# Attention sums with queries in the rows for the first two groups, dummy matmuls at the start, and a bank rule in the planner

## The chip, the cores and the metric

The kernel runs on one core of a Trainium2 chip. The time is that of the device, in microseconds, for one execution; the median of three runs before the change is 550.58 us (549.27 to 551.24). The engines are TensorE (PE, matmuls; its weight loads are shown as PEld), VectorE (DVE), ScalarE (ACT), GpSimd (POOL), and SyncE (SP), which only issues DMAs. PE writes to PSUM, eight banks that DVE and ACT can read and POOL cannot.

## The reference

Three parts follow one another. Window attention: 2 batches x 8 heads, 768 positions, 64 dimensions; a query sees the first 4 keys (sinks) and the 128 keys up to its own. Then a dense feed-forward layer over 1536 rows. Then a routed layer: eight experts, each row to its best one.

```python
scores = scale * np.matmul(q, k.transpose(0, 1, 3, 2))
keep = is_sink | in_window                       # pos < n_sink; 0 <= rel < window
scores = np.where(keep, scores, -1e9)
a = np.exp(scores - np.max(scores, axis=-1, keepdims=True))
a = a / (np.sum(a, axis=-1, keepdims=True) + 1e-09)
x = np.matmul(a, v)                              # then to rows of 512
h = x @ w_in; x = np.maximum(0.01 * h, h) @ w_out
# routed: softmax gate over 8 experts, argmax, x + gate * (relu(x @ w1[e]) @ w2[e])
```

## The kernel before

The 1536 rows are six groups of 256 (g = 0 to 5; 0 to 2 are the first batch). The attention of a group has eight items: four head pairs p times two query tiles qt of 128. The dense layer of a group is 16 chunks f: twelve matmuls of 256 columns (line 845), a leaky ReLU that goes ACT, DVE, ACT, DVE (lines 856 to 859), and six matmuls of 512 columns (line 866). The weights of the dense layer are read as raw words, decoded by DVE and split in two parts (lines 737 to 741, 701, 708) once, during group 0. While the chunks of a group run, the attention of the next one is worked in between. The routed part begins some 430 us into the run.

All work is written as operations with an engine, a cost, a priority `pr`, what they read and write, and the buffers that they hold. `Plan.run` goes through planned time with these costs and starts on each engine the ready operation of the best priority whose buffers fit; the resulting order is the program's order on each engine. Buffers have tags with a number of slots: for PSUM `acc` 2, `h` 2, `S` 1, `T` 2, `PV` 1. `T` takes whatever PE turns (keys `pk`, queries `pq`, probabilities `tt`). Plan.gap gives the time from one operation to one that depends on it.

Groups 0 and 1 (`self.whole`) work in full fp32; group 2 does so for the scores; the others split numbers in two parts. An item of group 0 or 1 runs like this, in `item`: the score matmul of each head (line 578) with queries `qz` that `prep` copied from the turned bank with the factor -0.125 (lines 465 on DVE, 468 on ACT; 454 and 456 are the keys and the sink keys); mask and minimum on DVE (line 585); exponential with its sum on ACT (line 588); the sum's reciprocal `sm` on DVE (592, 593); the probabilities are scaled by it, on ACT (line 597) in group 1 and for the second head in group 0, on POOL (line 600) for the first head in group 0; PE turns them (line 616, and 638 for the sink columns from the third query block on); ACT copies them to `AT` (line 620); and PE sums the values (line 655). There the weights are the values of a head, 64 columns beside 64 cleared ones (POOL clears them, line 365), the moving operand is the 128 turned probabilities, and the sum comes out with dimensions in the rows, as the dense layer wants it. ACT copies it (line 661), and DVE makes the second part (line 662). Where sinks count, each head has one matmul more, against `vs` (cleared on POOL, line 405).

The values are loaded by two DMAs a block, one for each head of the pairs (line 349), the keys and queries by one a block (line 343). In groups 3 to 5 the turned keys are copied by ACT and subtracted by DVE (lines 501 and 503), both for two heads.

Of the kernel before, what the change touches and what calls it, by code (L numbers as in the profile page):

```python
# [47 lines left out]
C_TR = 114.0  # L48
# [3 lines left out]
class Buf:  # L52
    __slots__ = ("tag", "shape", "dtype", "tile", "left", "state", "first", "loose")

    def __init__(self, tag, shape, dtype):
        self.tag, self.shape, self.dtype = tag, shape, dtype
        self.tile = None
        self.left, self.first = 0, 1 << 60
        self.state = {}


class Op:
    __slots__ = ("i", "eng", "cost", "fn", "pr", "after", "wait", "ready", "bufs", "lat", "start")


class Plan:
# [12 lines left out]
    def __init__(self, slots, any_order=()):  # L79
        self.any_order = any_order  # L80
# [16 lines left out]
    def op(self, eng, cost, fn, r=(), w=(), pr=0.0, lat=0.0, hold=(), after=()):  # L97
# [28 lines left out]
        for d in deps:  # L126
            d.after.append(o)
        bufs.update(dict.fromkeys(hold))
# [7 lines left out]
    def run(self, emit_alloc):  # L136
# [12 lines left out]
        def fits(o):  # L149
            need = {}  # L150
# [13 lines left out]
        while future:  # L164
# [18 lines left out]
            for eng in sorted(ready):  # L183
# [42 lines left out]
class Arm:  # L226
# [4 lines left out]
    def __init__(self, tc, io, cst, scr, xg, window_attention):  # L231
# [19 lines left out]
        self.p = Plan({**base, **attn, **late}, ("T", "acc"))  # L251
# [78 lines left out]
    def blocks(self, g, b, qp):  # L330
# [5 lines left out]
        def ld(t, a, p0, p1):  # L336
# [3 lines left out]
            if t != "v":  # L340
                eng, dma = ("ACT", nc.scalar) if g == 0 and t == "k" and p0 == 0 else ("SP", nc.sync)
                x = self.raws[t, a // 2]
                P.op(eng, C_DMA, lambda: dma.dma_start(
                    out=x.tile[:, a % 2, 128 * p0:128 * p1].rearrange("p (h d) -> p h d", d=64), in_=src.rearrange("h p d -> p h d")),
                    w=[(x, (a % 2, p)) for p in range(p0, p1)], pr=pr, lat=64 * n * 1024 / 200.0)
                return
            x = self.raws[t, a]
            for h in range(2):
                P.op("SP", C_DMA, lambda h=h: nc.sync.dma_start(
                    out=x.tile[:, p0:p1, h, 64 * h:64 * h + 64], in_=io["v"][b, 2 * p0 + h:2 * p1:2, 128 * a:128 * a + 128, :].rearrange("h p d -> p h d")),  # L350
                    w=[(x, (h, 0))], pr=pr, lat=32 * n * 1024 / 200.0)

        new = range(2 * qp, 2 * qp + 2)
        for t in "qk":
            self.raws[t, qp] = P.buf("w", [128, 2, 512])
        for p0, p1 in ((0, 1), (1, self.KD)) if g == 0 else ((0, self.KD),):
# [3 lines left out]
            if p0 == 0:  # L360
                for a in new:

                    x = self.raws["v", a] = P.buf("w", [128, self.KD, 2, 128])
                    for h in range(2):
                        P.op("POOL", 100 + 0.9 * 256, lambda x=x, h=h: nc.gpsimd.memset(x.tile[:, :, h, 64 - 64 * h:128 - 64 * h], 0.0), w=[(x, (h, 1))], pr=pr)
                    if g:
                        ld("v", a, 0, self.KD)
        if g == 0:
            for a in new:
                ld("v", a, 0, self.KD)  # L370
# [21 lines left out]
    def sinks_v(self, g, b, whole):  # L392
# [3 lines left out]
        vs = self.vs = P.buf("vs", [128, self.KD, 2, 128], F32 if whole else F32R)  # L396
        if whole:
            def ld():
                for h in range(2):
                    nc.sync.dma_start(out=vs.tile[h:32:2, :, h, 64 * h:64 * h + 64], in_=src(h))  # L400
# [4 lines left out]
            P.op("POOL", 1000, lambda: nc.gpsimd.memset(vs.tile, 0.0), w=[vs], pr=pr - 7)  # L405
# [27 lines left out]
    def prep(self, g, qp, p, whole):  # L433
# [21 lines left out]
        if qp == 0:  # L455
# [4 lines left out]
        P.op("PE", 2 * C_TR, lambda: [nc.tensor.transpose(pq.tile[:, j, :], flat("q", 2 * qp + j), idt) for j in range(2)],  # L460
             r=[part("q", 2 * qp + j) for j in range(2)], w=[pq], pr=pr, hold=[kT])
# [91 lines left out]
    def item(self, g, qp, p, qt, whole):  # L553
# [40 lines left out]
        for h in range(2):  # L594
            if g == 1 or g == 0 and h:

                P.op("ACT", c_act(ncol, False), lambda h=h: nc.scalar.activation(out=A.tile[:, 0:ncol, h], in_=A.tile[:, 0:ncol, h], func=AF.Copy, scale=sm.tile[:, h:h + 1]),
                     r=[sm], w=[(A, h)], pr=pr)
                continue
# [26 lines left out]
        if whole:  # L626
            vb = [self.raws["v", 2 * qp - 1 + j] for j in js]
            rd = [*AT, *vb]
            vblk = lambda i, h: vb[i].tile[:, p, h, :]
# [17 lines left out]

        def pvmm():
            for h in range(2):
# [3 lines left out]
                for n, (l, r) in enumerate(mm):  # L653
                    to = pv.tile[:, 0, 0:128] if whole else pv.tile[:, h, :]
                    nc.tensor.matmul(out=to, lhsT=l, rhs=r, start=n == 0 and not (whole and h), stop=n == len(mm) - 1 and (h == 1 or not whole))  # L655

        P.op("PE", (nj + 2 * sink) * (213 if whole else c_mm(256)), pvmm, r=rd, w=[pv], pr=pr)
        if whole:
            xT = self.xt[g]
            x = lambda i: xT.tile[:, i, p, 128 * qt:128 * qt + 128]  # L660
            P.op("ACT", c_act(128, True), lambda: nc.scalar.activation(out=x(0), in_=pv.tile[:, 0, 0:128], func=AF.Copy), r=[pv], w=[(xT, (p, 0, qt))], pr=pr)
            P.op("DVE", c_dve(128), lambda: nc.vector.tensor_tensor(out=x(1), in0=pv.tile[:, 0, 0:128], in1=x(0).bitcast(F32), op=ALU.subtract),
# [781 lines left out]
```

## Time and profile before

| | |
|---|---|
| median of three runs | 550.58 us |
| the profiled execution | 549.7 us |
| its span, first to last instruction | 548.0 us |
| PE busy | 517.1 us (94%) |
| DVE busy | 411.6 us (75%) |
| ACT busy | 344.3 us (63%) |
| POOL busy | 164.5 us (30%) |

The span is what the trace covers; the execution's own time is 1.7 us longer. Shares of busy time are averages over a start, a stretch with the weights' decoding, the other groups, and the routed part, and each has other limits. A matmul's end is modelled, so where PE reads full one looks at the distance from one start to the next. An fp32 matmul of groups 0 and 1 leaves two records.

### The profile page before, as it was taken

The page shows a single profiled execution, that of the slowest core. Times are in us where ns is not written, and L with a number is a line of the kernel's source. Part 1 is how long each engine was busy: PE and PEld are TensorE (multiplying, and loading weights), DVE is VectorE, ACT ScalarE, POOL GpSimd, SP SyncE. Part 2 cuts the span into 40 slices and gives each one's busy share as a digit, 9 for nine tenths or more (in the row PEclk, how much of TensorE's full clock was granted, in tenths as well). Part 3 has the DMA queues.
Part 4 walks back from the last instruction along what each step waited for, and adds up shares of the span by engine and source line. Part 5 has one row for each costly group of instructions (what it writes and reads, how often), then busy time and mean ns, then how long its engine had stood idle before and what let it go on. Part 6 is the DMA issues. An engine that isn't in the chain of part 4 may idle for free.

```text
span 548.0 us, 10288 instructions
## 1 busy us (share of the span) xinstructions
PE 517.1 (94%) x3341; PEld 452.8 (83%) x3341; DVE 411.6 (75%) x1168; ACT 344.3 (63%) x899; POOL 164.5 (30%) x288
## 2 busy tenths in 40 slices
PE   3889999999998999989999999999999999999994
PEld 2779899888887999878988889999998778888883
DVE  4889999998667677687777776675765587788781
ACT  3998865655576556676566676465656377765760
POOL 4332012230155134332433333211131033455331
PEclk9999999999999999999999999999999999999998
DMA  8998443630110211131112230104565359988750
GB/s 158 298 333 279 156 144 97 198 105 25 64 42 22 69 27 42 41 93 35 45 46 50 49 85 18 26 1 178 169 185 191 116 179 372 315 280 300 245 193 19
DMA packets 83806, 72.44 MB, mean 132 GB/s; under 512 B 56563, under 2 KB 64755, under 8 KB 83744
## 3 DMA queue, kind: packets, MB, share of 16 engines
q1 hardware_dynamic: 81456, 70.54, 42.3%
q0 software_dynamic: 1600, 1.04, 0.6%
q8 instruction: 28, 0.46, 0.3%
q14 instruction: 34, 0.28, 0.2%
q10 hardware_dynamic: 688, 0.13, 0.1%
HBM read 65.40 MB, written 10.51 MB: 139 GB/s over the span
## 4 chain that ended last, share of the span: by engine, by line
PE 74%; DVE 11%; ACT 7%; issue 3%; POOL 2%; DMA 2%; POOLq 0%; SPq 0%; ACTq 0%; DVEq 0%
PE h L845 19%; PE acc L866 15%; PE acc L1103 8%; PE h L1086 4%; PE PV L655 4%; PE T L616 3%; PE S L1086 2%; PE PV L1086 2%; PE S L582 2%; DVE C L671 2%; ACT P L588 2%; PE S L866 2%; PE PV L866 2%; DVE kT L503 1%; PE T L1096 1%
## 5 line engine op out<-in xcount | busy, mean ns | idle before, releaser
L845 PE MATMUL h<-x,w 128*128 128x256 f32 x1128 | 154.7, 286 | 0.3 <-DVE x L708 0.2
L845 PEld LDWEIGHTS h<-x,w 128*128 128x128 f32 x1128 | 144.1, 190 | 4.9 <-DVE w L708 0.6
L866 PE MATMUL acc<-w,gh 128*128 128x512 f32 x308 | 100.2, 406 | 0.0
L588 ACT ACTIVATE P<-P,s 128x272 f32<-128x272 f32 (+1 forms) x96 | 50.1, 523 | 27.6 <-DVE s L585 26.2
L600 POOL TENSOR_SCALAR P<-P,s 128x272 f32<-128x272 f32 (+1 forms) x72 | 36.6, 520 | 90.1 <-DVE s L593 77.4
L866 PE MATMUL acc<-w,gl 128*128 128x512 f32 x156 | 61.3, 393 | 0.0
L856 ACT ACTIVATE t<-h 128x256 f32<-128x256 f32 x94 | 35.6, 379 | 38.2 <-PE h L845 37.8
L866 PEld LDWEIGHTS acc<-w,gh 128*128 128x128 f32 x308 | 53.2, 189 | 7.6
L857 DVE TENSOR_TENSOR h<-h,t 128x256 f32<-128x256 f32 x94 | 40.2, 428 | 21.8 <-ACT t L856 21.2
L708 DVE TENSOR_TENSOR w<-wm,w 128x1024 fp32r<-128x1024 f32 x36 | 49.3, 1376 | 3.8 <-ACT w L701 3.2
L701 ACT ACTIVATE w<-wm 128x1024 fp32r<-128x1024 f32 x44 | 45.1, 1057 | 5.1 <-PE h L845 2.9
L859 DVE TENSOR_TENSOR gl<-h,gh 128x256 fp32r<-128x256 f32 x92 | 38.6, 419 | 10.2 <-ACT gh L858 8.9
L858 ACT ACTIVATE gh<-h 128x256 fp32r<-128x256 f32 x92 | 34.9, 379 | 17.4 <-DVE h L857 16.6
L585 DVE CUSTOM_DVE_ANT_0 P<-S,mk 128x272 f32<-128x272 f32 (+1 forms) x70 | 28.9, 413 | 14.7 <-PE S L582 10.2
L701 ACT ACTIVATE w<-wf 128x512 fp32r<-128x512 f32 x52 | 32.0, 626 | 11.1 <-DVE wf L741 8.8
L866 PEld LDWEIGHTS acc<-w,gl 128*128 128x128 f32 x156 | 29.3, 188 | 6.8 <-DVE gl L859 0.2
L708 POOL TENSOR_TENSOR w<-wm,w 128x1024 fp32r<-128x1024 f32 x8 | 19.7, 2461 | 41.8 <-ACT w L701 21.1
L616 PE MATMUL T<-idt,P 128*128 128x128 f32 x152 | 26.9, 293 | 3.8 <-DVE kT L503 2.9
L672 POOL TENSOR_TENSOR xr<-C 128x128 f32<-128x128 f32 x32 | 15.6, 488 | 47.2 <-DVE C L671 46.8
L708 DVE TENSOR_TENSOR w<-wf,w 128x512 fp32r<-128x512 f32 x42 | 28.8, 693 | 0.7 <-ACT w L701 0.7
L616 PEld LDWEIGHTS T<-idt,P 128*128 128x128 f32 x152 | 22.3, 205 | 8.5 <-issue 4.2
L622 ACT ACTIVATE AT<-T 128x256 fp32r<-128x256 f32 x60 | 20.1, 382 | 12.1 <-PE T L616 11.3
(274 smaller groups left out, 1105.9 us busy)
## 6 DMA issues: line engine op xcount, KB each, us to landing
wm<-in_moe_w_dram SPq DMA_DIRECT2D x44, 512.0 KB, 3.8
w<-in_moe_w_in_dram SPq DMA_DIRECT2D x14, 512.0 KB, 7.4
w<-in_moe_w_out_dram SPq DMA_DIRECT2D x14, 512.0 KB, 6.5
wf<-in_moe_w_dram SPq DMA_DIRECT2D x20, 256.0 KB, 4.4
vs<-in_moe_w_dram SPq DMA_DIRECT2D x10, 512.0 KB, 5.7
rq<-in_q_dram SPq DMA_DIRECT2D x56, 64.0 KB, 5.8
out_dram<-x SPq DMA_DIRECT2D x12, 256.0 KB, 2.5
rk<-in_k_dram SPq DMA_DIRECT2D x24, 96.0 KB, 2.2
```

What stands on the lines that cost most here:

```text
L588: P.op("ACT", 280 + 0.83 * ncol, lambda h=h: nc.scalar.activation(out=A.tile[:, 0:ncol, h], in_=A.tile[:, 0:ncol, h], func=AF.Exp, scale=- ...
L600: P.op("POOL", 245 + 0.83 * ncol, lambda h=h: nc.gpsimd.tensor_scalar(out=A.tile[:, 0:ncol, h], in0=A.tile[:, 0:ncol, h], scalar1=sm.tile[ ...
L616: nc.tensor.transpose(tt.tile[:, 2 * j + h, :], A.tile[:, o:o + 128, h], c["idt"])
L701: nc.scalar.activation(out=at(0), in_=view(src.tile), func=AF.Copy)
L708: P.op(lo, {"DVE": c_dve(n), "POOL": c_pool2(n)}[lo], lambda: eng[lo].tensor_tensor(out=at(1), in0=view(src.tile), in1=at(0).bitcast(F32), ...
L845: nc.tensor.matmul(out=h.tile, lhsT=wi.tile[:, a, 128 * k:128 * k + 128], rhs=xT.tile[:, b, k, :], start=k == 0 and n == 0, stop=k == self ...
L856: P.op("ACT", c_act(256, True), lambda: nc.scalar.activation(out=t.tile, in_=h.tile, func=AF.Copy, scale=0.01), r=[h], w=[t], pr=fast)
L857: P.op("DVE", c_dve(256), lambda: nc.vector.tensor_tensor(out=h.tile, in0=h.tile, in1=t.tile, op=ALU.max), r=[t], w=[h], pr=fast)
L859: P.op("DVE", c_dve(256), lambda: nc.vector.tensor_tensor(out=gl.tile, in0=h.tile, in1=gh.tile.bitcast(F32), op=ALU.subtract), r=[h, gh], ...
L866: nc.tensor.matmul(out=acc[i].tile, lhsT=a.tile[:, q], rhs=wo.tile[:, b, :], start=first and n == 0, stop=last and n == 2)
L1086: nc.tensor.matmul(out=hp[a].tile, lhsT=xt.tile[:, i, k, :], rhs=w1[k][j].tile[:, 512 * a:512 * a + 512], start=k == 0 and n == 0, stop=k ...
L1103: nc.tensor.matmul(out=yp.tile, lhsT=gt.tile[:, a, 2 * n + j, :], rhs=w2[n][b].tile[:, 512 * j:512 * j + 512], start=n == 0 and j == 0 and ...
```

## The change

In groups 0 and 1 the sums are made the other way round: the turned probabilities are the weights, the 64 value columns of a head are the moving operand, and the sum comes out with queries in the rows. One matmul of 128 columns adds the sinks of both heads. Since the queries are now in the rows, the reciprocal scales the sum (ACT, 64 columns a head) in place of the probabilities; PE turns the scaled sum, and copy and second part are made from there. Values need no cleared halves, so they are loaded by one DMA a block. In group 0's first pair ACT makes both query copies. PE gets seven dummy matmuls at the start and five behind the first turned queries. The planner holds back an operation from a PSUM buffer while another engine is planned at it, and a little beyond.

```diff
+        def fits(o):
+            if any(b.tag in self.banks and b.by != o.eng and b.until > now and b not in o.held for b in o.bufs):
+                return False
...
+                for b in got.bufs:
+                    if b.tag in self.banks and b not in got.held:
+                        b.by, b.until = eng, end + (195.0 if eng == "PE" else 150.0)
+                        later(b.until, "idle", None)
...
-        self.p = Plan({**base, **attn, **late}, ("T", "acc"))
+        self.p = Plan({**base, **attn, **late}, ("T", "acc"), self.psum_tags)
...
-        for t in "qk":
+        for t in "qkv":
             self.raws[t, qp] = P.buf("w", [128, 2, 512])
...
+        if g == 0 and p == 0:
+            self.warm(5, pr, [turned])
         for h in range(2):
-            if g == 0 and h:
+            if g == 0 and p and h:
                 P.op("DVE", c_dve(256), ...
...
-        for h in range(2):
-            if g == 1 or g == 0 and h:
-                P.op("ACT", c_act(ncol, False), ... scale=sm.tile[:, h:h + 1]
-                continue
+        for h in [] if whole else range(2):
             P.op("POOL", 245 + 0.83 * ncol, ...
...
+        def rows():
+            mm = [(pv.tile[:, 0, 0:128], wz.tile, vs.tile[:, p, :])] if sink else []
+            mm += [(pv.tile[:, 0, 64 * h:64 * h + 64], at(i, h), vblk(i, h)) for h in range(2) for i in range(len(js))]
+            for n, (to, l, r) in enumerate(mm):
+                nc.tensor.matmul(out=to, lhsT=l, rhs=r, start=n == 0, stop=n == len(mm) - 1)
...
-        P.op("PE", (nj + 2 * sink) * (213 if whole else c_mm(256)), pvmm, r=rd, w=[pv], pr=pr)
+        P.op("PE", (nj + sink) * 222 if whole else (nj + 2 * sink) * c_mm(256), rows if whole else pvmm, r=rd, w=[pv], pr=pr)
         if whole:
+            y = P.buf("qT", [128, 128])
+            def scale():
+                for h in range(2):
+                    nc.scalar.activation(out=y.tile[:, 64 * h:64 * h + 64], in_=pv.tile[:, 0, 64 * h:64 * h + 64], func=AF.Copy, scale=sm.tile[:, h:h + 1])
+            P.op("ACT", 2 * c_act(64, True), scale, r=[pv, sm], w=[y], pr=pr)
+            tx = P.buf("T", [128, 128])
+            P.op("PE", C_TR, lambda: nc.tensor.transpose(tx.tile, y.tile, c["idt"]), r=[y], w=[tx], pr=pr)
...
+        if self.fast:
+            self.spare = self.p.buf("acc", [128, 512])
+            self.warm(7, -100)
...
+    def warm(self, n, pr, after=()):
+        nc, ones, x = self.nc, self.c["ones"], self.spare
+        many = ones.rearrange("p (o n) -> p o n", o=1).to_broadcast([128, 4, 128])
+        self.p.op("PE", 10 * n, lambda: [nc.tensor.matmul(out=x.tile.rearrange("p (o n) -> p o n", o=4), lhsT=ones, rhs=many, start=True, stop=True) for _ in range(n)],
+                  w=[x], pr=pr, after=after)
```

The rule changes the planned times and with them the order on all engines, up to the routed part; behind it the order is the same. Three places follow, each before and after. In the rows a tile's number stands behind its name.

PE, from the start to the first turned probabilities, before (keys and queries `w` are turned into `T`; `S` and `h` take scores; `acc` takes turned probabilities):

```order
L450 MATMUL T_151<-idt,w_127 128x128 x2
L460 MATMUL T_155<-idt,w_131 128x128 x2
L578 MATMUL S_171<-kT_152,w_141 128x128
L578 MATMUL h_176<-kT_152,w_141 128x128
L578 MATMUL h_181<-kT_152,w_141 128x272
L578 MATMUL S_188<-kT_152,w_141 128x272
```

The same after; `acc_129` takes the dummies:

```order
L814 MATMUL acc_129<-ones 128x512
L442 MATMUL T_154<-idt,w_127 128x128 x2
L452 MATMUL T_158<-idt,w_139 128x128 x2
L814 LDWEIGHTS ones
L814 MATMUL acc_129<-ones 128x512
...
L572 MATMUL S_175<-kT_155,w_152 128x128
L572 MATMUL h_180<-kT_155,w_152 128x128
L572 MATMUL h_183<-kT_155,w_152 128x272
L572 MATMUL S_192<-kT_155,w_152 128x272
```

Seven dummies stand ahead of the first turning and five between the queries' turning and the first score.

PE in group 1 before, one item's sum and the work behind it (`PV` is the sum, `AT` the turned probabilities, `w_242` and `w_261` the values, `C` and `vs` the sinks, `h` a chunk of the dense layer):

```order
L655 MATMUL PV_1017<-AT_987,w_242 128x128
L655 MATMUL PV_1017<-AT_987,w_261 128x128
L655 MATMUL PV_1017<-C_129,vs_148 128x128
L655 MATMUL PV_1017<-AT_987,w_242 128x128
L655 MATMUL PV_1017<-AT_987,w_261 128x128
L655 MATMUL PV_1017<-C_129,vs_148 128x128
L578 MATMUL S_1033<-kT_760,w_141 128x272
L845 MATMUL h_1042<-x_251,w_984 128x256 x12
L616 MATMUL T_1060<-idt,P_956 128x128 x4
L638 MATMUL T_1067<-idt,P_956 32x128
```

After (`qT_986` is the scaled sum):

```order
L642 MATMUL PV_967<-vs_141,C_137 128x128
L642 MATMUL PV_967<-w_150,AT_901 128x64
L642 MATMUL PV_967<-w_252,AT_901 128x64
L642 MATMUL PV_967<-w_150,AT_901 128x64
L642 MATMUL PV_967<-w_252,AT_901 128x64
L605 MATMUL T_977<-idt,P_909 128x128 x4
L627 MATMUL T_990<-idt,P_909 32x128
L572 MATMUL S_992<-kT_813,w_152 128x272
L859 MATMUL h_998<-x_281,w_934 128x256 x12
L664 MATMUL T_1020<-idt,qT_986 128x128
```

Five matmuls take the place of six, and the scaled sum is turned behind the next probabilities, a score and a chunk.

PE in a later group before, from a turning of keys to the third turning, which takes the keys' bank again (`rk` keys, `rq` queries, `P` probabilities; `T` has two slots):

```order
L494 MATMUL T_3428<-idt,rk_3224 128x128 x3
L681 MATMUL T_3436<-idt,rq_3363 128x128 x2
L866 MATMUL acc_2582<-w_1820,gh_3391 128x512 x2
L866 MATMUL acc_2582<-w_1820,gl_3394 128x512
L866 MATMUL acc_2583<-w_1820,gh_3391 128x512 x2
L866 MATMUL acc_2583<-w_1820,gl_3394 128x512
L845 MATMUL h_3462<-x_3432,w_367 128x256 x3
L616 MATMUL T_3470<-idt,P_3375 128x128 x4
```

After:

```order
L488 MATMUL T_3441<-idt,rk_3229 128x128 x3
L685 MATMUL T_3449<-idt,rq_3347 128x128 x2
L880 MATMUL acc_2724<-w_1741,gh_3411 128x512 x2
L880 MATMUL acc_2724<-w_1741,gl_3415 128x512
L880 MATMUL acc_2725<-w_1741,gh_3411 128x512 x2
L880 MATMUL acc_2725<-w_1741,gl_3415 128x512
L859 MATMUL h_3473<-x_1962,w_1899 128x256 x12
L605 MATMUL T_3488<-idt,P_3393 128x128 x4
```

Here twelve matmuls of a chunk stand ahead of the third turning in place of three.

## Rows read from the trace of the kernel before

**Rows 1.** The page: busy time by engine, and tenths in 40 slices
```profile
PE 517.1 (94%) x3341; PEld 452.8 (83%) x3341; DVE 411.6 (75%) x1168; ACT 344.3 (63%) x899; POOL 164.5 (30%) x288
...
PE   3889999999998999989999999999999999999994
```

**Rows 2.** Stretches: length, busy us (instructions) by engine, clock, DMA share, GB/s
```profile
0.00:10.00 10.00, 2.02 (x7) 1.38 (x8) 3.59 (x15) 2.32 (x5) 6.16 (x26) 1.00 0.80 140
...
20.00:30.00 10.00, 8.48 (x59) 7.09 (x59) 9.46 (x37) 8.91 (x31) 3.49 (x7) 1.00 1.21 295
...
60.00:70.00 10.00, 10.00 (x71) 9.20 (x70) 9.70 (x29) 8.12 (x24) 0.22 (x1) 1.00 0.09 36
```

**Rows 3.** Timeline of PE at the start: start, us, instruction [idle before, its end]
```profile
9.33 0.77 PE L578 MATMUL S<-kT,w 128*128 128x128 f32 x2 [2.19 <-ACT w L468]
...
11.23 1.11 PE L578 MATMUL S<-kT,w 128*128 128x272 f32 x2
...
13.71 0.52 PE L616 MATMUL acc<-idt,P 128*128 128x128 f32 x2 [0.89 <-POOL P L600]
...
16.19 0.62 PE L578 MATMUL S<-kT,w 128*128 128x272 f32 x2
```

**Rows 4.** Timeline of the other engines at the start
```profile
2.24 0.19 POOL L1368 MEMSET ones<- 128x128 bf16 x1
...
7.03 0.18 ACT L456 ACTIVATE ks<-T 128x16 f32<-128x16 f32 x1
...
8.35 0.43 DVE L465 TENSOR_SCALAR w<-T 64x256 f32<-64x256 f32 x1
8.81 0.38 ACT L468 ACTIVATE w<-T 64x256 f32<-64x256 f32 x1 [1.60 <-DVE w L465]
...
10.47 0.41 ACT L588 ACTIVATE P<-P,s 128x128 f32<-128x128 f32 x1 [1.28 <-DVE s L585]
...
11.95 0.55 ACT L588 ACTIVATE P<-P,s 128x272 f32<-128x272 f32 x1 [0.55 <-DVE s L585]
...
17.89 0.41 DVE L737 TENSOR_SCALAR wf<-w 128x512 int32<-128x512 int32 x1
```

**Rows 5.** The chain that ended last: start, us, what
```profile
56.49 1.39 PE acc L866 x6
57.88 1.34 PE PV L655 x12
...
140.92 0.87 PE T L929 x8
```

**Rows 6.** Timeline of PE: fp32 records with 128 and with nine columns
```profile
57.72 0.61 PE L655 MATMUL PV<-AT,w 128*128 128x128 f32 x4
...
146.65 0.61 PE L951 MATMUL T<-fold,wl 18*128 18x9 f32 x4
```

**Rows 7.** ACT's groups to 95 us: count, busy us, mean ns, idle before
```profile
L597 ACT ACTIVATE P<-P,s 128x272 f32<-128x272 f32 x20 | 10.1, 544 | 1.2 <-DVE s L593 1.1
...
L661 ACT ACTIVATE x<-PV 128x128 fp32r<-128x128 f32 x16 | 4.2, 265 | 3.9 <-PE PV L655 3.9
...
L597 ACT ACTIVATE P<-P,s 128x128 f32<-128x128 f32 x4 | 1.6, 400 | 0.0
...
L456 ACT ACTIVATE ks<-T 128x16 f32<-128x16 f32 x4 | 0.7, 170 | 0.0
```

**Rows 8.** PE's waits at 120 to 440 us: total, times, longest
```profile
PE T L616 <- DVE kT L503: 2.9, 7, 0.6
...
PE T L638 <- DVE qT L684: 1.3, 4, 0.6
```

**Rows 9.** Timeline around two turnings of keys, at 239 and 302 us
```profile
239.60 0.71 PE L616 MATMUL T<-idt,P 128*128 128x128 f32 x4 [0.61 <-DVE kT L503]
...
301.85 0.98 ACT L501 ACTIVATE kT<-T 64x384 fp32r<-64x384 f32 x2
...
302.87 1.12 DVE L503 TENSOR_TENSOR kT<-T,kT 64x384 fp32r<-64x384 f32 x2
```

More of the change, by code (lines that the diff above doesn't have):

```diff
@@ L52 @@
 class Buf:
-    __slots__ = ("tag", "shape", "dtype", "tile", "left", "state", "first", "loose")
+    __slots__ = ("tag", "shape", "dtype", "tile", "left", "state", "first", "loose", "by", "until")
     def __init__(self, tag, shape, dtype):
@@ L58, in __init__ @@
         self.left, self.first = 0, 1 << 60
+        self.by, self.until = None, 0.0
         self.state = {}
 class Op:
-    __slots__ = ("i", "eng", "cost", "fn", "pr", "after", "wait", "ready", "bufs", "lat", "start")
+    __slots__ = ("i", "eng", "cost", "fn", "pr", "after", "wait", "ready", "bufs", "lat", "start", "held")
 class Plan:
@@ L339, in ld @@
             src = io[t][b, heads, 128 * a:128 * a + 128, :]
[L340 to L347, printed above, removed]
-            for h in range(2):
-                P.op("SP", C_DMA, lambda h=h: nc.sync.dma_start(
-                    out=x.tile[:, p0:p1, h, 64 * h:64 * h + 64], in_=io["v"][b, 2 * p0 + h:2 * p1:2, 128 * a:128 * a + 128, :].rearrange("h p d -> p h d")),
-                    w=[(x, (h, 0))], pr=pr, lat=32 * n * 1024 / 200.0)
+            eng, dma = ("ACT", nc.scalar) if g == 0 and t == "k" and p0 == 0 else ("SP", nc.sync)
+            x = self.raws[t, a // 2]
+            P.op(eng, C_DMA, lambda: dma.dma_start(
+                out=x.tile[:, a % 2, 128 * p0:128 * p1].rearrange("p (h d) -> p h d", d=64), in_=src.rearrange("h p d -> p h d")),
+                w=[(x, (a % 2, p)) for p in range(p0, p1)], pr=pr, lat=64 * n * 1024 / 200.0)
         new = range(2 * qp, 2 * qp + 2)
-        for t in "qk":
+        for t in "qkv":
             self.raws[t, qp] = P.buf("w", [128, 2, 512])
@@ L359, in blocks @@
                     ld(t, a, p0, p1)
[L360 to L370, printed above, removed]
+        for a in new:
+            ld("v", a, 0, self.KD)
     def load(self, g, b, qp, p):
@@ L459, in prep @@
             out=snk(), in0=ks(), scalar1=1.0, scalar2=1.0, op0=ALU.mult, op1=ALU.mult), r=[("ks", p)], w=[(kT, "s")], pr=pr)
[L460 to L461 removed]
+        turned = P.op("PE", 2 * C_TR, lambda: [nc.tensor.transpose(pq.tile[:, j, :], flat("q", 2 * qp + j), idt) for j in range(2)],
+                      r=[part("q", 2 * qp + j) for j in range(2)], w=[pq], pr=pr, hold=[kT])
+        if g == 0 and p == 0:
+            self.warm(5, pr, [turned])
         for h in range(2):
             rows, key = slice(64 * h, 64 * h + 64), [(self.qz, (p % 2, h))]
[L464 removed]
+            if g == 0 and p and h:
                 P.op("DVE", c_dve(256), lambda rows=rows, h=h: nc.vector.tensor_scalar(
@@ L653, in pvmm @@
                 for n, (l, r) in enumerate(mm):
-                    to = pv.tile[:, 0, 0:128] if whole else pv.tile[:, h, :]
-                    nc.tensor.matmul(out=to, lhsT=l, rhs=r, start=n == 0 and not (whole and h), stop=n == len(mm) - 1 and (h == 1 or not whole))
-        P.op("PE", (nj + 2 * sink) * (213 if whole else c_mm(256)), pvmm, r=rd, w=[pv], pr=pr)
+                    nc.tensor.matmul(out=pv.tile[:, h, :], lhsT=l, rhs=r, start=n == 0, stop=n == len(mm) - 1)
+        P.op("PE", (nj + sink) * 222 if whole else (nj + 2 * sink) * c_mm(256), rows if whole else pvmm, r=rd, w=[pv], pr=pr)
         if whole:
```

26 lines of the change are left out of this document (12 added, 14 removed).

## The prediction

> **What bounds the kernel now.** I read the busy line and the slices first [rows 1], then the same by stretch [rows 2]. TensorE (PE) is busy for 517.1 of 548.0 us, and its slices read 9 from about 14 us to the end. A busy PE is not yet a bound, so the chain comes next [rows 5]: from 56 us on it is one PE row after another at the pace of full work (6 matmuls of 512 columns in 1.39 us, 0.23 each). In that stretch VectorE (DVE) is full as well: 9.70 of 10 us at 60 to 70 us, with PE at 10.00 [rows 2]. Before it lies the start: PE does 2.02 us of work in the first 10 us and 8.48 in 20 to 30, while ScalarE (ACT) and DVE stand at 8.91 and 9.46 [rows 2]. So two things can shorten the run: less PE work anywhere after 40 us, or an earlier start for all three engines.
>
> **PE work of the sums.** Before, a sum in group 1 is six matmuls of 128 columns in 1.34 us, 0.223 each [rows 5]; each leaves two records, 0.112 apart. After, four of them stream 64 columns, one (the sinks) streams 128, and one turning is added. Does 64 cost half of 128? The trace has no 64-column matmul of this type, but it has both sides: four records with 128 columns take 0.61 us, and four with nine columns take 0.61 us too [rows 6]. The records go at the pace of their 128 weight columns, not of what they stream. So 64 columns cost 0.224, as 128 do; this is the end I take, since nine lies beyond 64 on the small side. A turning costs 0.109 (eight in 0.87 [rows 5]). Group 1: 8 items, each -0.223 + 0.109, is -0.91. Group 0 has no sinks there: 8 items at +0.109 are +0.87. The sum is **0.0 us**. Bounds: if 64 columns did take half, 56 matmuls x 0.112 = -6.3; the other end is +0.5, if each turning waited some 0.03 more for its weights.
>
> **The start.** The first score matmul begins at 9.33, 2.19 after the turning before it, and waits for ACT's query copy [rows 3]. That copy began at 8.81 because it waited 1.60 for DVE's copy out of the same bank, which stood behind DVE's masks until 8.35 [rows 4]. After, ACT makes both copies, right behind the sink keys that end at 7.03 + 0.18 = 7.21: 7.21 + 2 x 0.38 = 7.97, and the score starts at about 8.1, **-1.2**. DVE loses 0.43 there, ACT gains 0.38.
>
> Two score matmuls of 272 columns take 1.11 us at 11.23 and 0.62 at 16.19 [rows 3]: the engine runs at the lower of its two levels (1.2 GHz) until about 12.3 us, though the clock column reads 1.00 [rows 2]; I go by the durations. The twelve new dummy matmuls stand ahead of and between the turnings of the keys and queries and the first scores. The ones that they read are filled at 2.24 + 0.19 = 2.43 [rows 4]; seven at half pace are 7 x 0.46 = 3.2 us (0.23 at full pace [rows 5], doubled), done at 5.7, when the first keys come. The five behind the queries take 1.2 us at full pace and end with ACT's copies, or 2.3 at half pace, and then the first score starts at 9.4 and the 1.2 above is gone. Before, the pace rose while the first scores ran; after, the dummies and the turnings have run ahead of those scores, so I take the full pace for them. The four scores of the first two items then take 1.4 instead of 2.8. Of this, ACT sees its two waits before the third and fourth exponentials (0.55 at 11.95 [rows 4], and one like it) go, about 0.8.
>
> So ACT's exponentials begin at about 9.0 instead of 10.47, and its lead is 1.5 + 0.8 = 2.3 us by the fourth. PE then no longer waits for POOL's scaling (0.89 at 13.71 [rows 3]); what is late next is the exponential on ACT, since it is ACT that fills up from 14 us on.
>
> **ACT's own account.** Removed: in group 0, four scalings of 128 and four of 272 columns (0.40 and 0.54, in all 3.8 us); in group 1, sixteen of 272 (8.7 us) [rows 7]. Added: two scalings of 64 columns out of PSUM per item, 16 in each group. The nearest rows are the 128-column copy from PSUM, 0.265, and the 16-column one, 0.17 [rows 7]; the upper end is 0.40, the 128-column scaling by a column of factors. I take 0.27, the copy's, as fewer columns and the factor weigh against each other: 4.3 us a group. Group 0: -3.8 + 4.3 + 0.38 = +0.9 (bounds -0.7 to +3.0); group 1: -4.4, on an engine that is not the bound there. The Trainium skill (ScalarE: Activation LUTs, section What ACT_TABLE_LOAD costs) gives a factor read from a column as some 93 ns more than a constant; by that page a scaling would be an estimated 0.24 to 0.33, and group 0's account +0.4 to +1.9. No row here has the 64-column form.
>
> The lead that arrives at PE's full stretch is 2.3 - 0.9 = 1.4, plus some 0.4 for PE's waits on POOL that go: **-1.8** (bounds -3.5 to 0).
>
> **Where the rest goes.** POOL loses eight clears and eight scalings; it stood idle before those scalings. On SyncE's queue the values' DMAs of a group go from four to two with the same pieces, so they land when they did; DVE reads the first weights only at 17.89 [rows 4], behind its attention work. Both at 0; without that cover a weight that lands half a microsecond later costs as much. The turned sum takes a T bank and the scaled one a query slot, which group 2's queries wait for; those are wanted only once group 1's sums are done.
>
> **The bank rule.** ACT's two copies of the turned keys take 0.98 us from 301.85, and DVE's subtraction, which needs only the first, starts after both, at 302.87 [rows 9]. So the program already keeps the engines apart; the old plan counts them as overlapping and sends PE to the bank too early. The price of that between 120 and 440 us is 2.9 us in 7 waits and 1.3 in 4 [rows 8]. How much does the new order cover? At the place shown, where PE waited 0.61 at 239.60 [rows 9], nine more matmuls (9 x 0.12) now stand before the bank's next use, so that wait goes. But most other turnings of keys have the same cover in both orders, and their waits of 0.3 to 0.45 stay. I take **-0.8** (bounds: -4.2 if all go; +2 if the new order opens as many new ones as it had).
>
> **Sum** against the profiled run's own 549.7 us: -1.8 + 0.0 - 0.8 = -2.6, so 547.1. That run is 0.9 under the median of the three, 550.58; on it the forecast is **548.0**. Faster or slower by 0.3% means under 548.9 or over 552.2, about what a measurement of this kernel can tell from no change.
>
> **Rivals.**
> *The lead is lost in group 0.* If a 64-column scaling takes 0.40, ACT gets 3.0 us more in group 0, which is more than the lead of 2.3; or the five dummies run at half pace and the first score stays at 9.3. Then only the bank rule is left: about 550.2. For it: ACT is at 8.91 of 10 at 20 to 30 us [rows 2]. Against: group 1 gives ACT 4.4 back.
> *64 columns cost half.* Then PE has 6.3 us less to do and the time is about 542. Against it stand the nine-column records [rows 6]. The Trainium skill (TensorE: Matmul & The Clock Gate, section Back-to-back issue gap) has the spacing of matmuls fall with the columns streamed; by that rule this rival holds, and the trace, 0.61 us for either four, speaks against it.
> *The plan recovers most of the bank waits.* Another -2.5, about 545.5. For it: all of them have one cause [rows 8, 9].
> *Slower: PE stands at the turned sums.* PE works in order; behind the turning stand scores and chunks, which DVE and ACT then get later. A scaled sum needs 2 x 0.27 us on ACT and two handovers. In the new order PE has 0.4 us of work between sum and turning in four items of group 0, but 1.1 us or more in most of group 1. If ACT is in an exponential (0.6 to 0.75 us with its accumulator) when the sum is ready, the turning waits that much more. It decides from (2.6 + 1.6) / 16 = 0.27 us of wait per turning on the bounding path; at 0.5 per turning the time is 548.0 + 8.0 = 556, at 0.35 some 553.6. Against it: in group 0 PE is not the bound.
>
> **How the numbers follow.** Forecast (546.3 to 549.6): 0.46, of which 0.09 lies within 0.3%. Lead lost (549.8 to 551.5): 0.21. Most waits recovered (544.5 to 546.3): 0.15. Half price at 64 columns: 0.05. Slower: 0.13. Faster 0.37 + 0.15 + 0.05 = 0.57; same 0.30; slower 0.13. The range 544.5 to 551.5 leaves out the 0.05 and the 0.13.
>
> **What would show it.** Right: the first score at about 8.1 us with 0.62 for two of 272 columns; records of the 64-column sums 0.11 apart; PE work before the routed part unchanged within 0.3 us; the 0.61 wait gone. Wrong: 64-column records nearer than 0.08 (second rival); ACT scalings of 0.4 us (first); waits of 0.3 us or more at many turned sums in group 1 (fourth).

## The result, and the profile after

The changed kernel takes 545.58 us (median of 11 executions, 542.75 to 547.99) against 550.72 of the kernel before on the same chip (11 executions, 549.03 to 552.05): a ratio of 0.9898, with a 95% interval of 0.9871 to 0.9924, so 1.0% faster. The forecast was 548.0, faster by over 0.3%, with a range of 544.5 to 551.5. The time lies in the range and the sign is right; the size is twice what was forecast, and the sections below show that two terms were far off and that one loss was not foreseen. The executions of the changed kernel spread with the mean granted clock that each shows, from 542.75 us at 0.997 to 547.99 at 0.986; the profile is of one with 0.997 (542.75 us, span 541.0).

The page of the changed kernel, its busy line, PE's slices and the chain by engine:

```profile
PE 516.1 (95%) x3353; PEld 451.2 (83%) x3353; DVE 412.0 (76%) x1167; ACT 340.9 (63%) x908; POOL 158.0 (29%) x272
...
PE   7989999999998899999999999999999999999994
...
PE 78%; DVE 10%; ACT 6%; issue 2%; POOL 1%; DMA 1%; ACTq 0%; POOLq 0%; DVEq 0%
```

Against [rows 1] the total hardly moves, though the dummies are in it now; the start reads 7 and 9 where it read 3 and 8. Around 170 us one slice read 8 before; now two side by side do, from 162 to 189 us. The stretches of the changed kernel show more (length, then busy us by engine):

```profile
160.00:180.00 20.00, 15.99 (x114) 13.72 (x112) 14.04 (x46) 12.86 (x40) 8.56 (x20) 1.00 0.15 46
```

and the same stretch of the kernel before:

```profile
160.00:180.00 20.00, 18.18 (x117) 16.13 (x118) 14.63 (x47) 12.58 (x40) 9.73 (x23) 1.00 0.14 32
```

PE is busy there, at the end of group 1's chunks, for 15.99 of 20 us where it was 18.18. The timeline of PE at the start, to be read against [rows 3]:

```profile
2.49 3.17 PE L814 MATMUL acc<-ones 128*128 128x512 bf16 x7 [2.49 <-POOL ones L1382]
...
6.66 1.24 PE L814 MATMUL acc<-ones 128*128 128x512 bf16 x5
7.74 0.39 PE L572 MATMUL S<-kT,w 128*128 128x128 f32 x2
...
8.66 0.62 PE L572 MATMUL S<-kT,w 128*128 128x272 f32 x2
...
13.85 1.00 PE L642 MATMUL PV<-w,AT 128*128 128x64 f32 x8
```

Seven dummies take 3.17 us, 0.45 each, the five behind them 0.25 each: by these durations PE has gone from the lower of its two levels (1.2 and 2.4 GHz) to the upper one between the two groups, though the clock column reads 1.00 over the whole start. The first score starts at 7.74 instead of 9.33, and the first pair with 272 columns takes 0.62 instead of 1.11. Eight records of a sum with 64 columns take 1.00, the last of them its full 0.28, so they lie 0.10 apart on average, 0.11 behind the first step, like those of 128 and nine columns in [rows 6]. The timeline of ACT over the same time, against [rows 4, 7]:

```profile
6.99 0.78 ACT L462 ACTIVATE w<-T 64x256 f32<-64x256 f32 x2
8.50 0.41 ACT L582 ACTIVATE P<-P,s 128x128 f32<-128x128 f32 x1 [0.73 <-DVE s L579]
...
9.91 0.52 ACT L582 ACTIVATE P<-P,s 128x272 f32<-128x272 f32 x1
...
13.11 0.52 ACT L660 ACTIVATE qT<-PV,s 128x64 f32<-128x64 f32 x2
```

and ACT's fourth exponential in the kernel before:

```profile
12.86 0.53 ACT L588 ACTIVATE P<-P,s 128x272 f32<-128x272 f32 x1 [0.28 <-DVE s L585]
```

Both query copies run back to back, and the exponentials begin at 8.50 instead of 10.47. By the fourth, at 9.91 instead of 12.86, ACT's lead has grown to 2.95 us. The two scalings of 64 columns take 0.52 together, 0.26 for each, since they overlap; each lasts 0.31.

### The profile page after: what moved, and what is told of

It is laid out like the page before. It is cut to its first block, busy times and chain, and to the rows that moved or that the text cites. A ratio compares the mean times of both kernels' runs of the same rounds, so it can differ in the third digit from the quotient of the medians.

```text
span 541.0 us, 10282 instructions
## 1 busy us (share of the span) xinstructions
PE 516.1 (95%) x3353; PEld 451.2 (83%) x3353; DVE 412.0 (76%) x1167; ACT 340.9 (63%) x908; POOL 158.0 (29%) x272
## 4 chain that ended last, share of the span: by engine, by line
PE 78%; DVE 10%; ACT 6%; issue 2%; POOL 1%; DMA 1%; ACTq 0%; POOLq 0%; DVEq 0%
PE h L859 21%; PE acc L880 18%; PE acc L1117 8%; PE h L1100 4%; PE T L605 4%; PE PV L650 2%; PE PV L1100 2%; PE S L1100 2%; PE S L576 2%; PE PV L642 2%; ACT P L582 1%; PE S L572 1%; PE T L1110 1%; DVE P L579 1%; DVE kT L497 1%
## 5 line engine op out<-in xcount | busy, mean ns | idle before, releaser
L589 POOL TENSOR_SCALAR P<-P,s 128x272 f32<-128x272 f32 (+1 forms) x64 | 32.0, 515 | 75.0 <-DVE s L587 61.0
L1024 POOL DMA_INDIRECT scr<-x,sm x12 | 13.3, 1109 | 50.5 <-ACT wl L963 16.0
```

## The experiments

The kernel before ran 11 times beside each set, with medians of 550.54 to 550.75. Each row below: what the kernel has, its median, and the ratio to the kernel before with its 95% interval.

| kernel | sums in rows | start (dummies, ACT's copies) | bank rule | leads | us | ratio |
|---|---|---|---|---|---|---|
| changed kernel | yes | yes | yes | 10, 5 | 545.58 | 0.9898 (0.9871 to 0.9924) |
| e1_norule | yes | yes | no | 10, 5 | 547.70 | 0.9942 (0.9928 to 0.9956) |
| e2_nodummies | yes | copies | yes | 10, 5 | 545.49 | 0.9907 (0.9888 to 0.9927) |
| e3_oldsums | no | yes | yes | 10, 5 | 541.82 | 0.9856 (0.9834 to 0.9877) |
| e4_ruleonly | no | no | yes | 10, 5 | 545.51 | 0.9915 (0.9901 to 0.9930) |
| e5_startonly | no | yes | no | 10, 5 | 547.49 | 0.9946 (0.9927 to 0.9965) |
| e6_rowsonly | yes | no | no | 10, 5 | 548.13 | 0.9962 (0.9949 to 0.9975) |
| e7_g2_12 | yes | yes | yes | 12, 5 | 539.74 | 0.9809 (0.9792 to 0.9827) |
| e8_g2_9_6 | yes | yes | yes | 9, 6 | 538.40 | 0.9784 (0.9767 to 0.9802) |
| e9_nodummies | yes | copies | yes | 9, 6 | 539.38 | 0.9800 (0.9781 to 0.9818) |
| e10_dveq | yes | dummies | yes | 9, 6 | 538.43 | 0.9784 (0.9766 to 0.9802) |
| e12_norule | yes | yes | no | 9, 6 | 545.21 | 0.9903 (0.9880 to 0.9926) |

"Leads" are the two numbers in the plan's `order` by which the attention of group 2, and of groups 3 to 5, is due before the chunks that it must be ready for; e11_after is the changed kernel once more. Where the expectations give 6.0 and 1.3 us for PE's standing at 170 to 180 us, these are added up from the distances between the starts of its matmuls; the busy column of the same 10 us leaves 4.01 and 0.48, since a matmul's modelled end covers part of a pause. Such sums depend on what one takes as an undisturbed row; differences between kernels depend on it much less.

**The rule alone, and the rest without it.** e1_norule takes this line out of the changed kernel; e4_ruleonly puts the rule, this line and those in `fits`, into the kernel before:

```diff
-        self.p = Plan({**base, **attn, **late}, ("T", "acc"), self.psum_tags)
+        self.p = Plan({**base, **attn, **late}, ("T", "acc"))
```

> The changed kernel with the plan's bank rule taken out; sums in rows, dummies and the first query copies stay. Theory 1 (the start carries most: its marks in the trace stand 3.2 to 3.6 us earlier by the third to the seventh chunk): about 547.4 against 550.7 of the kernel before, so the rule is worth 1.8. Theory 2 (the rule carries most, since the waits at banks between 120 and 440 us fell): 549 or more. The record's own step (rule 0.8): 546.4. The border of groups 1 and 2, where PE stood 6.0 us in the changed kernel against 1.3 before (170 to 180 us): if the rule's new order opened it, PE stands under 2 us there; if the new sums did, it stays near 6.

> The kernel before with the bank rule in its plan and nothing else. The record's step (the rule covers the 0.61 wait and little else): 549.9. Theory 2 (it recovers most of the waits at banks): about 547.3. Third (the new order opens as many waits as it closes): 550.7 or more, with other waits named in 120 to 440 us. At the border of groups 1 and 2 (170 to 180 us) PE stands 6 us if the rule's order opened that gap, 1.3 if not.

The rule alone brings 550.75 to 545.51, -5.2, where the record had -0.8. That is even more than the second theory of e4 gave, but the reason given there, that most of the waits at banks go, does not carry it. PE's waits for the copies of turned keys and queries were 2.9 and 1.3 us before [rows 8]. In e4_ruleonly, at 120 to 440 us (total, times, longest), they are:

```profile
PE T L624 <- DVE kT L511: 1.9, 6, 0.5
...
PE S L590 <- DVE qT L692: 0.4, 1, 0.4
```

All waits that the profile names there fall from 8.5 to 6.4 us, by 2.1 where the time falls by 5.2. So what the rule is worth is shown, and where in the order it saves it is not. Taken from the changed kernel it seems worth 2.1 only, as the first theory of e1 had it. And neither kernel has the gap: PE is busy for 9.96 (e1) and 10.00 (e4) of the 10 us from 170 to 180. So the gap needs the rule and something else.

**The sums alone, the start alone.** e6_rowsonly has the new sums and the values' loads, and neither rule, dummies nor ACT's copies. e5_startonly has the old sums and this:

```diff
+        if g == 0 and p == 0:
+            self.warm(5, pr, [turned])
         for h in range(2):
-            if g == 0 and h:
+            if g == 0 and p and h:
...
+        if self.fast:
+            self.spare = self.p.buf("acc", [128, 512])
+            self.warm(7, -100)
```

> The kernel before with the sums of the first two groups in rows and scaled there, and nothing else: no bank rule, no dummies, the first pair's second query copy on DVE. The record's steps: PE's work unchanged (64 columns cost what 128 do), ACT +0.5 in the first group, PE's waits on POOL's scaling gone (-0.4): about 550.8. Rival A (64 columns cost half): 544.5. Rival B (PE stands at the turned sums, 0.35 a piece): 555. Theory 3 (the values' loads or the missing scaling on POOL shorten the start beyond the lead of the first scores): 549 or less.

> The kernel before with the dummies and with ACT making both query copies of the first pair, and nothing else: old sums, no bank rule. The record's step for the start without what the sums bring (first score -1.2, scores at the full clock, of which ACT sees 0.8, then PE waits on POOL's scaling again): 549.2. Rival (ACT and POOL's scaling are the bound of the first group, the earlier scores only wait longer): 550.7, and POOL's waits before the first turned probabilities grow over 0.89. First score at 7.7 us, two of 272 columns in 0.62, in either case.

e5 leaves PE's order as it was but for the twelve dummies, so marks can be laid side by side. The timeline of PE in the kernel before, the second product of two early chunks:

```profile
43.56 0.83 PE L866 MATMUL acc<-w,gh 128*128 128x512 f32 x2
...
56.12 0.83 PE L866 MATMUL acc<-w,gh 128*128 128x512 f32 x2
```

and in e5_startonly the same two, behind its first score:

```profile
7.70 0.38 PE L580 MATMUL S<-kT,w 128*128 128x128 f32 x2
...
40.86 0.83 PE L878 MATMUL acc<-w,gh 128*128 128x512 f32 x2
...
53.43 0.82 PE L878 MATMUL acc<-w,gh 128*128 128x512 f32 x2
```

PE's waits in e5 from 0 to 60 us (total, times, longest), the longest one behind the dummies:

```profile
PE acc L618 <- POOL P L602: 2.3, 3, 1.1
```

Both marks are 2.70 us earlier, and the time is 3.0 less: the start arrives whole, more than the 1.3 that the record's steps gave for it without the sums. The rival, that POOL's scaling would eat it, is refuted: PE waits 2.3 us for it in three waits, as long as in the kernel before, and the lead passes through.

e6 gains 2.6 where 0 was expected, and the first reason stands on POOL and DVE. The timeline of the kernel before, two DVE operations on the masks and what POOL does beside them:

```profile
5.16 0.74 DVE L1378 TENSOR_SCALAR scratch<-scratch 128x128 f32<-128x128 f32 x1
...
7.53 0.45 DVE L1390 COPY mk<-scratch 128x16 f32<-128x16 f32 x1
...
4.86 0.94 POOL L405 MEMSET vs<- 128x1024 f32 x1
...
7.39 0.30 POOL L458 TENSOR_SCALAR kT<-ks 128x32 f32<-128x32 f32 x1 [0.88 <-ACT ks L456]
```

The same two operations in e6, its DVE query copy and its first score:

```profile
5.20 0.22 DVE L1380 TENSOR_SCALAR scratch<-scratch 128x128 f32<-128x128 f32 x1
...
6.99 0.17 DVE L1392 COPY mk<-scratch 128x16 f32<-128x16 f32 x1
...
7.53 0.43 DVE L457 TENSOR_SCALAR w<-T 64x256 f32<-64x256 f32 x1
...
8.51 0.77 PE L570 MATMUL S<-kT,w 128*128 128x128 f32 x2 [1.33 <-ACT w L460]
```

Before, a DVE operation that takes 0.22 by itself took 0.74 and ended 0.10 after POOL's clear; a copy of 0.17 took 0.45 beside POOL's work from 7.39 on. In e5, which keeps the clears, the first of them takes 0.76. With the new sums the clears of the values are gone, and the one of `vs` is half as big and over at 3.2 us. So in e6 POOL is idle while the masks are made, and they end 0.8 us earlier; DVE's query copy begins at 7.53 instead of 8.35 [rows 4], and the first score at 8.51 instead of 9.33. The Trainium skill has this (SBUF — State Buffer, section Who interferes with whom): DVE in certain modes and GpSimd share one pair of ports as an exclusive lock, and the one that comes second is fully blocked until the first has finished. The trace agrees, 0.74 against 0.22. That these operations run in such a mode is not shown here, and not every one waits: those beside POOL's next two clears, from 5.75 to 6.51 us, take what they take in e6.

What else the sums bring is not settled. By the medians they add nothing to the start: e5 has 547.49, e1 with both 547.70. The traces of the profiled executions say otherwise. The timeline of PE, the last matmul of group 1's chunks, in the kernel before, e6, e5 and e1:

```profile
179.45 0.39 PE L866 MATMUL PV<-w,gl 128*128 128x512 f32 x1
177.47 0.39 PE L868 MATMUL PV<-w,gl 128*128 128x512 f32 x1
176.77 0.39 PE L878 MATMUL PV<-w,gl 128*128 128x512 f32 x1
174.64 0.39 PE L880 MATMUL PV<-w,gl 128*128 128x512 f32 x1
```

With the sums it comes 2.0 us earlier alone and 2.1 on top of the start, and of these 1.9 are left at the last chunk of all (426.47 against 428.36). But the executions of e1 reach from 545.66, the profiled one, to 548.28, and those of e5 from 545.76 to 548.40, and that hides a difference of this size.

**Old sums with rule and start.** e3_oldsums puts the sums, the scaled probabilities and the values' loads of the kernel before into the changed one.

> The changed kernel with the kernel before's sums of the first two groups put back (values in the rows, probabilities scaled, values loaded into cleared blocks); bank rule, dummies and ACT's first query copies stay. If the parts add up (the sums alone were worth 2.3 to 2.6 us): 547.9, the time goes up by the sums' share. If the gap at the border of groups 1 and 2 (PE stood 6.0 us in 170 to 180 us in the changed kernel, 1.3 before, and neither the rule alone nor the sums alone had it) comes only from rule and sums together: PE stands under 2 us there, which gives back up to 4 us, and the time is 544 to 546. The record's step (the sums are worth 0.0): 545.6.

It is *faster* than the changed kernel, 541.82 against 545.58. PE is busy for 9.43 of the 10 us from 170 to 180: no gap. So by the medians the new sums cost 3.8 us here, not by their own work but by what the plan makes of them together with the rule. The changed kernel's median holds executions with a low clock, however: the two profiled executions, at 0.995 and 0.997, differ by 1.2 (541.54 and 542.75). Between e5 and e3, which differ by the rule alone, stand 5.7 us. PE's waits at 120 to 440 us (total, times, longest), in e5:

```profile
PE T L618 <- DVE kT L505: 2.5, 7, 0.5
PE T L955 <- DVE wl L945: 1.3, 1, 1.3
PE T L640 <- DVE qT L686: 1.3, 4, 0.6
PE T L496 <- issue: 1.2, 1, 1.2
```

and in e3:

```profile
PE h L865 <- DVE gl L879: 1.3, 2, 1.1
PE T L626 <- DVE kT L513: 1.1, 3, 0.5
...
PE T L648 <- DVE qT L694: 0.5, 1, 0.5
```

All four stand ahead of matmuls into a `T` bank, 6.3 us together, and 1.6 of these are left with the rule. But others come in their place, 1.3 at the chunks (gl) and several under 1 us, and the whole list falls from 7.5 to 6.8 us only; so here too the named waits do not carry the 5.7. The two for the copies of keys (kT) and queries (qT) are those of [rows 8]. The two others stood in the same list with the same times and were not counted: 1.3 for the second part of what the gating's logits are made from (wl, a wait for data and not for a bank), and 1.2 at the first turned keys of group 3, for which the profile names no releaser.

**The gap, and two versions that close it.** The timeline of PE there, in the changed kernel:

```profile
171.87 0.74 PE L605 MATMUL T<-idt,P 128*128 128x128 f32 x4 [0.73 <-DVE sAT L631]
...
174.25 0.63 PE L943 MATMUL T<-idt,x 128*128 128x128 f32 x4 [1.41 <-DVE AT L612]
...
175.07 0.40 PE L650 MATMUL acc<-AT,vhl 128*128 128x256 f32 x2
...
180.58 0.58 PE L965 MATMUL T<-fold,wl 18*128 18x9 f32 x4 [1.16 <-DVE qT L688]
```

Group 1's last chunk ends at 171.1. The last probabilities of group 2's attention are turned only behind it, at 171.87, and summed at 175.07; group 2's chunks need that sum and begin at 181.09. Between, PE has only short steps, and the longest pauses are waits for DVE. e7 changes one number, e8 two:

```diff
-        return 16 * (g - 1) + 4 * p + 2 * qt - (21 if g < 2 else 10 if g == 2 else 5)
+        return 16 * (g - 1) + 4 * p + 2 * qt - (21 if g < 2 else 12 if g == 2 else 5)
```

> The changed kernel with the third group's attention two steps earlier in the plan (10 becomes 12); no instruction more or less. Theory (the gap at the border of groups 1 and 2 comes from attention that the plan leaves too late, and sets the end): PE stands about 2 us in 160 to 180 us in place of 7.1, and the time is 542 to 543. Rival (the standing only moves to a later stage or another wait): 545.6 with the sum of PE's standing unchanged. On the granted clock: executions of the changed kernel differ by it (0.997 with 542.8 us, 0.986 with 548.0); if the gap at the border brings the fall, these executions lie close together (0.995 or more in all); if not, they spread as before.

> The changed kernel with the third group's attention one step later (10 becomes 9) and that of the fourth to sixth one step earlier (5 becomes 6). Theory (each border of two groups has its own best lead; the new leads let the plan close the gap at the first border and the waits near 280 us): 541 to 543. Rival (what the plan counts and what the chip does differ by more than such a step): 544 to 547, with other waits at 220 to 300 us.

The same place in e7:

```profile
170.41 0.40 PE L650 MATMUL acc<-AT,vhl 128*128 128x256 f32 x2
...
174.98 0.44 PE L576 MATMUL S<-kT,qT 128*128 128x128 f32 x2 [0.47 <-DVE s L579]
175.26 2.01 PE L859 MATMUL h<-x,w 128*128 128x256 f32 x15
```

and its stretch:

```profile
160.00:180.00 20.00, 19.35 (x140) 17.12 (x139) 14.55 (x48) 12.79 (x40) 7.89 (x18) 1.00 0.19 54
```

The last sum stands at 170.41, ahead of the last chunk's second product (171.35 to 172.9), and group 2's chunks follow at 175.26. PE is busy for 19.35 of 20 us, and the time is 539.74: 5.8 us below the median of the changed kernel and 3.0 below its fastest execution, the one that was profiled. e8 goes on to 538.40, the fastest of all, 2.2% under the kernel before; its PE is busy for 256.10 of the 260 us from 180 to 440, e7's for 254.64. Both are faster than their theories had them. In e7 group 2's attention is due two steps earlier than in the changed kernel, in e8 one step later, and e8's border is closed as well (19.33 of 20 us busy). So it is not an early lead as such that closes the gap, but the order that the plan falls into with it. Which of e8's two numbers does it, and what other leads would do for the old sums, was not run.

**What in the start does it.** e2_nodummies and e9_nodummies cut the two groups of dummies to one matmul of 128 columns each (e2 in the changed kernel, e9 in e8); e10_dveq puts the first pair's second query copy back on DVE:

```diff
-            if g == 0 and p and h:
+            if g == 0 and h:
```

> The changed kernel, instruction for instruction, with each of the two groups of dummy matmuls (seven and five of 512 columns) cut to one of 128. Theory 1 (dummies raise the clock before the first scores): the first four score groups run at the lower level again, 0.22 a record instead of 0.11 for 128 columns and 1.1 instead of 0.62 for two of 272; the first score still near 7.7, since it waits for ACT's copies; ACT's exponentials later by 0.5 to 1.0, and the time up by about that, 546.4. Rival (ACT is the bound of the start and covers it): the records slow down, but the time stays at 545.6.

> The kernel with the new leads (9 and 6), with its two groups of dummy matmuls cut to one of 128 columns each and nothing else moved. In the changed kernel itself the spread of its executions hid what the dummies are worth (545.5 without, 545.6 with). Theory (the first scores run at the lower level without them, ACT's third and fourth exponentials wait 0.56 and 0.26 us, and the start is PE's and ACT's): 538.4 + 0.8 to 1.4, 539.2 to 539.8. Rival (the first group's later work covers it): 538.4.

> The kernel with the new leads (9 and 6), with the first pair's second query copy on DVE again, behind its masks. The record's step: the first score comes 1.2 us later (near 8.9 in place of 7.7) and the time goes up by about that, 539.6. Rival (DVE's masks now end earlier than they did, since POOL and DVE have less to clear, so DVE's copy waits for nothing): under 0.4, 538.8 or less. Third (DVE's copy splits the work over two engines): faster than 538.4.

In e2 the medians hide the answer. Executions at the same granted clock, 0.997, show it: 543.98 to 544.41 us without the dummies, 542.75 to 542.96 with them. Against e8 the dummies are worth 1.0 us (539.09 to 539.64 without, 537.94 to 539.06 with). The timeline of e9, PE's fourth and last early score and ACT's third exponential:

```profile
9.62 1.11 PE L572 MATMUL S<-kT,w 128*128 128x272 f32 x2
...
10.35 0.55 ACT L582 ACTIVATE P<-P,s 128x272 f32<-128x272 f32 x1 [0.56 <-DVE s L579]
```

The pair takes 1.11 again, and ACT waits 0.56, as in [rows 4]. The copy on ACT is worth nothing here (538.43), as the rival had it. The timeline of e10, PE's first score and DVE's query copy:

```profile
8.16 0.39 PE L572 MATMUL h<-kT,w 128*128 128x128 f32 x2
...
7.41 0.43 DVE L459 TENSOR_SCALAR w<-T 64x256 f32<-64x256 f32 x1
```

DVE copies at 7.41, not at 8.35 [rows 4]; the first score comes 0.4 later than with ACT's copies, which the first group covers. By this the copy should matter only where POOL's clears hold DVE, and the new sums take those away; the copy alone, with the old sums, was not run.

**The rule with good leads, and the clock.**

> The kernel with the new leads (9 and 6) and no bank rule. Theory (the rule is worth 4.9 us where the border has no gap, as it was in the kernel before): 543.3, with the waits for the copies of turned keys back at 2.5 to 3.0 us in 120 to 440 us. Rival (the leads, not the rule, are what these kernels gain by, and the rule only shifted the order): under 540.5. The record's step (0.8): 539.2.

> The changed kernel once more, for a profile of one of its executions with a lower granted clock (0.986 to 0.989 in 6 of 11, 3 to 5 us longer). Theory (the fall begins where PE stands, at 170 to 180 us, and the matmuls behind it take twice as long for some microseconds): 0.986 to 0.990, the granted clock under 1.00 in one stretch right behind 170 us and 1.00 in the others before 440. Rival (the fall lies at the start or in the last part, as it does in the kernel before): the stretch from 160 to 200 us at 1.00. If the execution is one of 0.997, 542.8 us, nothing follows.

Without the rule and with e8's leads the time is 545.21: the rule is worth 6.8 us. Without the rule the leads bring 547.70 to 545.21, so they are no substitute. The sign that the theory named did not come: the waits for the copies of turned keys are 1.7 us in e12, not 2.5 to 3.0. The lists of named waits do not show that much: PE's at 120 to 440 us add up to 5.0 us in e12 and 4.6 in e8. The distances between the starts of PE's matmuls, each less what its kind takes in an undisturbed row, add up over the whole run to some 55 us of pauses in e12 and 47 in e8, and more than half of these 8 us lie between 180 and 280 us. Pauses over 0.6 us make 4.9 of them, shorter ones the rest. Why the rule saves more with these leads than alone, and which bank each short pause belongs to, stays open.

e11 gave 542.99 us at 0.997, so nothing follows from it for the clock.

## Why the prediction was right, point by point

**PE work of the sums, 0.0: right.** The 64-column records lie as far apart as those of 128, so the rival in which they cost half falls. The spacing by columns streamed, which the prediction cites beside it from the Trainium skill (TensorE: Matmul & The Clock Gate, section Back-to-back issue gap), is not what these records show. On top of the start the sums change the median by 0.2 (e5 to e1), and the profiled execution by 1.6 the other way. The wait of 0.61 is gone too, a sign that the prediction named: the longest of its kind in the changed kernel is 0.4.

**The start, -1.8: too small, its mechanism right.** First score 8.1 forecast, 7.74 measured; 0.62 for the pair; ACT's scaling 0.27 forecast, 0.26 measured. ACT's lead by the fourth exponential was forecast as 2.3 and is 2.95. In e5 2.70 of such a lead is left at the chunks, and the time is 3.0 less; start and sums together gave 3.0 as well (e1). So two terms were mis-sized. The lead was one. The other is ACT's own account, +0.9 in group 0: no run shows that it cost this time, since e5 loses nothing by the copy and e1, with the scalings too, is not slower than e5 beyond its spread. "POOL loses eight clears ... both at 0" needs a condition. Beside ACT's copies the clears do cost nothing (first score at 7.70 with them in e5, at 7.74 without). Alone they held DVE's masks by 0.8 us, and so they made the late query copy that the argument began with. The step took DVE's start at 8.35 [rows 4] as given and did not ask what the masks ahead of it were waiting for. Two slips carry no weight: PE's slices read 8, not 9, from 14 to 41 us [rows 1], and the first rival, with the bank rule alone, adds up to 549.8, not 550.2.

**The bank rule, -0.8: too small by a factor of six to nine.** Measured: -5.2 alone, -5.7 on top of the start, -6.8 with good leads. The failed step is the measure: the term was what the listed waits at banks could give back, "-4.2 if all go". In e4 six of the seven waits for turned keys are still there, 1.9 of 2.9 us, much as "their waits of 0.3 to 0.45 stay" had it, and the time falls by 5.2 all the same. Over the whole run PE's named waits fall by 2.1 us in e4, by 1.4 from e5 to e3 and by 3.3 from e12 to e8, so more than half of what the rule gives stands in none of them, and -4.2 was no bound. In which pauses it does stand is open. The time, 545.58, lies where the rival "the plan recovers most of the bank waits" had it, with 0.15; its reason, that these waits go, is not what e4 shows.

**What was not foreseen: the gap, +3.0 at equal granted clock and +5.8 by medians.** Rule and new sums together let group 2's attention end behind group 1's last chunk (no run has these two without the start). The rule's term had "+2 if the new order opens as many new ones as it had", but as waits at banks, not as a stretch in which PE runs out of chunks. So the forecast is near by luck, since errors of opposite sign partly cancel: about -3.0 for the start and -5.2 to -5.7 for the rule, less 3.0 to 5.8 for the gap, against -1.8 and -0.8.

**The slower rival falls.** PE's waits at the turned sums in the changed kernel, from 0 to 60 us (from 60 to 100 us, where the last ones run, there is none):

```profile
PE T L664 <- ACT kT L446: 0.5, 1, 0.5
...
PE T L664 <- ACT qT L660: 0.2, 1, 0.2
```

0.7 us in all over 16 turnings, where 0.27 at each would have decided. By the starts of PE's matmuls the pauses ahead of the 16 turnings add up to less than 2 us, which is still under half of that.

## What to carry to other kernels

Where a planner sets the order, a change of its rules or of a few operations moves work at every border of two stages; look there first for a stretch in which the bounding engine runs out of work, and tune the lead again before judging the change: here one number was worth 3.0 to 5.8 us, where the change as a whole brought 5.1 by the medians. A named wait is a bad bound for what a new order can give: more than half of what the rule gave stood in no list of waits. Take the parts apart in both directions, since each of the three parts alone had another price than in company. And an operation of the trace that takes three times as long as its like is a term of its own: ask which engine worked beside it.

## What the runs showed of the hardware

A DVE operation on 128x128 numbers took 0.74 us instead of 0.22 while POOL cleared 128x1024, and ended 0.10 us after it; in e5, beside the same clear, it took 0.76.

Fp32 matmuls with 128 weight columns left their records 0.11 us apart in undisturbed rows, with 64 columns streamed (changed kernel) as with 128 and with nine [rows 6].

The mean granted clock differed between executions of one kernel on one chip: 0.986 to 0.997 for the changed kernel, with 548.0 to 542.8 us, and 0.995 to 0.997 for e7 and e8, which lie within 0.8 and 1.1 us. That the gap brings the fall would fit these, but e12_norule has no gap (18.72 of 20 us busy at 160 to 180) and spreads too, 0.991 to 0.997 with 546.6 to 543.5 us. Nor does the clock order the times everywhere: e1 has 547.70 us at 0.997 and 545.66 at 0.995. No execution with a clock under 0.995 was profiled, so where in the run the clock falls stays open.
